# A chunked linear-attention stage fed into a SiLU feed-forward on one core: bonus sums, row casts and state rows reordered in the first six units, 128-column state sums, last rows in two halves

## The chip, the core and the metric

The kernel runs on one core of one Trainium2 chip. Its engines work side by side and meet at semaphores: TensorE (PE; its weight loads are shown apart, as PEld), VectorE (DVE), ScalarE (ACT), GpSimd (POOL) and SyncE (SP), which here only issues transfers. POOL issues transfers too, with a queue of its own. The metric is device microseconds of an execution, the median of several.

## What is computed

For each of 4 batches and 8 heads a 48x48 state runs over 768 time steps; its outputs, put side by side over the heads, go through a feed-forward of 384 to 2048 to 384 with a SiLU:

```python
for t in range(S):
    cur = einsum('bhd,bhe->bhde', u * k_t, v_t)
    y[:, :, t] = einsum('bhd,bhde->bhe', r_t, state + cur)
    state = w[..., None] * state + einsum('bhd,bhe->bhde', k_t, v_t)
x = y as (3072 rows, 384)
h = x @ w_in
out = (h * (1 / (1 + exp(-h)))) @ w_out
```

## The kernel before, in words

The 768 steps are cut into six chunks of 128; a unit is one chunk of one batch, so there are 24 units, unit i being chunk i // 4 of batch i % 4. Inside a unit the recurrence is written with matrices: r is multiplied by powers of w (lamR), k by inverse powers (lamK), both transposed so that the head dimension lies on partitions; a product of the two, masked to the strictly earlier steps, is multiplied by v; the state left by the chunks before is added by one more matmul; and the term with u (the bonus) is a row sum of r*k*u times v.

The names, in the order of a unit's work (lines of the kernel before):

- `nat_v` (L173, ACT) casts v to half precision. `nat_ku` (L178), `nat_rk` (L184) and `nat_kc` (L189), all on POOL, make k*u, r*k*u and k times w to the power of the steps left (lamC). `bonus_sum` (L195, DVE) sums r*k*u over the head dimension into rku, `bonus_vu` (L201, POOL) multiplies v by it. `bonus_act` (L205) is the same product done on ACT in eight pieces; nothing calls it in the kernel before.
- `p1` transposes r and k on PE into the PSUM tiles tr and tk (L221); DVE multiplies them by lamR and lamK into rk (L224, L228). From unit 4 on this is split in two: `p1t` (L240, into xs) and `p1d` (L251).
- `r16` (L257, ACT) casts the scaled r to half precision, for the matmul with the state.
- `p2` multiplies the two (L265 and L267, ae and ao, for even and odd heads); DVE masks both into am (L274). With `nxt` it also runs `p1t` of the next unit behind its matmuls and `p1d` behind its masks.
- `p3y` (L288, L291) makes y on PE, `p3e` (L298, DVE) adds vu; `p4` (L340) transposes y into yT, and ACT copies it into xT (L341).
- `sums` (L307) multiplies kc and v16 into the chunk's own state, sps. `state` (L316, L319 on DVE) adds it to the decayed one, and POOL makes sdec (L323) and, later, the half-precision state (L321). In chunks 0 and 1 that cast is `half_state` (L328, ACT).
- `l1` (L352, L355) is a tile of 128 hidden columns: three matmuls into hps, then a SiLU on ACT into gT. `l2` (L364) is a quarter of the 16 matmuls that make 128 rows of the output; behind the fourth quarter DVE copies (L368) and SP stores (L370).
- `to_cols` and `to_rows` turn a row of w or u into columns and spread columns over 128 rows. lamCT (L411, ACT) is turned into lamC by `to_rows`. `spin` issues matmuls on zeros.

Each engine runs its instructions in the order of the code, which is written out by hand. Units 0 to 5 are written one by one (L407 to L545), units 6 to 23 by the loop at L547. The feed-forward is cut into a list of fillers; `fill(n)` takes about n weights' worth from it (an `l1` over four batches or an `l2` quarter counts 1, an `l1` over two batches 0.5) and puts them between a unit's steps, so that PE has work while other engines finish. The last `fill(1000)` empties the list.

Transfers: SP loads r, k and v of each unit in 192 KB pieces, six units' worth of buffers. POOL issues w_in in four parts (L398) and w_out in two (L402); a memset into the buffer of unit 4 (L443), behind the last parts of w_in in POOL's queue, holds back the loads of unit 4 and all behind them. PSUM has five buffers for the attention's tiles, taken in turn, and three for hps and ops.

Of the kernel before, what the change touches and what calls it, by code (L numbers as in the profile page):

```python
# [8 lines left out]
FP = mybir.dt.float32  # L9
# [6 lines left out]
def kernel(  # L16
# [110 lines left out]
    def to_cols(row, copy):  # L127
        t = ps.tile([128, 512], FP, name="cols", tag="t", bufs=5)
        nc.tensor.transpose(t[0:PR, 0:NP], row.rearrange("p j d -> p (j d)")[:, 0:PR],
                            ident[0:NP, 0:NP])  # L130
        c = cst.tile([PR, NP], FP, name="cols_sb", bufs=2)
        copy(out=c, in_=t[0:PR, 0:NP])
        return c

    spin(5)
    wT = to_cols(wrow, nc.vector.tensor_copy)
    spin(5)
    u_bc = cst.tile([128, H, D], FP)
    lamC = cst.tile([128, H, D], FP)
# [1 line left out]
    def to_rows(dst, cols):  # L141

        t = ps.tile([128, NP, 2, 64], FP, name="rows", tag="t", bufs=5)
        for p in range(NP):
            nc.tensor.transpose(t[:, p, :, :].rearrange("t j d -> t (j d)")[:, 0:PR],
                                cols(p), ident[0:PR, 0:PR])
        nc.scalar.copy(out=dst.rearrange("t (p j) d -> t p j d", j=2), in_=t[:, :, :, 0:D])  # L147
# [22 lines left out]
    def nat_v(i):  # L170
        L = live.setdefault(i, {})
        L["v16"] = wrk.tile([128, H, D], F16, name="v16", bufs=6)
        nc.scalar.copy(out=L["v16"], in_=vin[i % NIN])  # L173
# [13 lines left out]
    def nat_kc(i):  # L187
        n = i % NIN
        nc.gpsimd.tensor_tensor(out=kc[i % NKC][:, :, 0:D], in0=kin[n][:, :, 0:D],  # L189
                                in1=lamC, op=ALU.mult)  # L190

    def bonus_sum(i):
        L = live[i]
        L["rku"] = wrk.tile([128, H], FP, name="rku", bufs=3)
        nc.vector.tensor_reduce(out=L["rku"], in_=L["rku_f"], axis=mybir.AxisListType.X,  # L195
                                op=ALU.add)

    def bonus_vu(i):
        L = live[i]
        L["vu"] = wrk.tile([128, H, D], FP, name="vu", bufs=3)  # L200
        nc.gpsimd.tensor_tensor(out=L["vu"], in0=vin[i % NIN],  # L201
                                in1=L["rku"].unsqueeze(2).broadcast_to([128, H, D]),
                                op=ALU.mult)
# [8 lines left out]
    def p1(i, mid=None, spins=0):  # L212
        n = i % NIN
        L = live.setdefault(i, {})
        tr = ps.tile([128, NP, C], FP, name="tr", tag="t", bufs=5)
        tk = ps.tile([128, NP, C], FP, name="tk", tag="t", bufs=5)
        spin(spins, tr)
        for t, src in ((tr, rin), (tk, kin)):
            flat = src[n].rearrange("p h d -> p (h d)")
            for p in range(NP):  # L220
                nc.tensor.transpose(t[0:PR, p, :], flat[:, 128 * p:128 * p + PR], ident)  # L221
        rk = wrk.tile([PR, 2, NP, C], FP, name="rk")
        L["rT"] = rk[:, 0]
        nc.vector.tensor_tensor(out=L["rT"], in0=tr[0:PR], in1=lamR, op=ALU.mult)  # L224
        if mid:
            mid()
        L["kT"] = rk[:, 1]
        nc.vector.tensor_tensor(out=L["kT"], in0=tk[0:PR], in1=lamK, op=ALU.mult)  # L228
# [27 lines left out]
        L["rT16"] = wrk.tile([PR, NP, C], F16, name="rT16")  # L256
        nc.scalar.copy(out=L["rT16"], in_=L["rT"])  # L257

    def p2(i, spins=0, nxt=None):
        L = live[i]  # L260
        ae = ps.tile([128, NP, C], FP, name="ae", tag="t", bufs=5)
        ao = ps.tile([128, NP, C], FP, name="ao", tag="t", bufs=5)
        spin(spins, ae)
        for p in range(NP):
            nc.tensor.matmul(ae[:, p, :], L["kT"][0:D, p, :], L["rT"][0:D, p, :],  # L265
                             start=True, stop=True)
            nc.tensor.matmul(ao[:, p, :], L["kT"][64:PR, p, :], L["rT"][64:PR, p, :],  # L267
                             start=True, stop=True)
        if nxt is not None:
            p1t(nxt)  # L270
        L["am"] = []
        for a in (ae, ao):
            am = wrk.tile([128, NP, C], F16, name="am", bufs=4)
            nc.vector.tensor_tensor(out=am, in0=a,  # L274
                                    in1=maskM.unsqueeze(1).broadcast_to([128, NP, C]),
                                    op=ALU.mult)
            L["am"].append(am)
        if nxt is not None:
            p1d(nxt)

    def p3y(i):
        sc, b = unit(i)
        L = live[i]
        v16 = L["v16"]
        L["y"] = y = ps.tile([128, H, D], FP, name="y", tag="t", bufs=5)
        for p in range(NP):
            if sc:
                nc.tensor.matmul(y[:, 2 * p:2 * p + 2, :], L["rT16"][:, p, :],  # L288
                                 st16[b][:, p, :], start=True, stop=False)
            for j in range(2):  # L290
                nc.tensor.matmul(y[:, 2 * p + j, :], L["am"][j][:, p, :],  # L291
                                 v16[:, 2 * p + j, :], start=not sc,
                                 stop=(not sc or j == 1))

    def p3e(i):
        L = live[i]
        L["y16"] = wrk.tile([128, H, D], F16, name="y16")
        nc.vector.tensor_tensor(out=L["y16"], in0=L["y"], in1=L["vu"], op=ALU.add)  # L298

    def sums(i):  # L300
        sc, b = unit(i)
        L = live[i]
        L["sps"] = sps = ps.tile([128, NP, PW], FP, name="sps", tag="t", bufs=5)
        kf = kc[i % NKC].rearrange("p h d -> p (h d)")
        vf = L["v16"].rearrange("p h d -> p (h d)")
        for p in range(NP):
            nc.tensor.matmul(sps[0:PR, p, :], kf[:, 128 * p:128 * p + PR],  # L307
                             vf[:, PW * p:PW * p + PW], start=True, stop=True)

    def state(i):  # L310
# [48 lines left out]
    def l2(sc, b, part):  # L359
# [6 lines left out]
        if part == 3:  # L366
# [2 lines left out]
            tt = b * S + sc * C  # L369
            nc.sync.dma_start(out=out[tt:tt + C, :], in_=osb)  # L370

    def l1s(sc, b0=0, b1=B):
        return [((b1 - b0) / B, lambda ft=ft: l1(sc, ft, b0, b1)) for ft in range(NFT)]

# [7 lines left out]
    def fill(n):  # L382
        owed[0] = min(owed[0] + n, n + 1.0)
        while fillers and owed[0] > 0.01:
            w_, f = fillers.pop(0)
            owed[0] -= w_
            f()
# [9 lines left out]
    def win_part(c0, c1):  # L397
        nc.gpsimd.dma_start(out=win[:, :, c0:c1],  # L398
                            in_=moe_w_in[:, c0:c1].rearrange("(q p) n -> p q n", p=128))
# [17 lines left out]
    nat_ku(0)  # L417
    nat_rk(0)
    p2(0)
    to_rows(lamC, lambda p: lamCT[:, p, :])  # L420
    bonus_sum(0)
    nat_ku(1)
    bonus_vu(0)
    nat_rk(1)
    p1(1, spins=3)
    p3y(0)
    p3e(0)
    nat_v(1)
    bonus_sum(1)
    win_part(512, 1024)  # L430
    bonus_vu(1)
    nat_kc(0)
    p2(1, spins=2)
    nc.scalar.copy(out=st[1], in_=zero)
    p4(0)
    p3y(1)
    p3e(1)
    p1(2)
    nat_ku(2)
    nat_rk(2)  # L440
# [7 lines left out]
    fillers.extend(l1s(0, 0, 2))  # L448
    fill(.5)
    nat_v(2)  # L450
    p2(2)
    bonus_sum(2)
    bonus_vu(2)
    nat_kc(1)
    fill(1.5)
    p3y(2)
    p3e(2)
# [2 lines left out]
    p4(2)  # L460
    nat_ku(3)
    nat_rk(3)
    nat_kc(2)
    nat_v(3)
    fill(1)
    p2(3)
    bonus_sum(3)
    bonus_vu(3)
    nc.scalar.copy(out=st[3], in_=zero)
    fill(2)  # L470
    p3y(3)
    p3e(3)
    a, b_ = B, B + 1
# [19 lines left out]
    fill(1)  # L493
    sums(0)
    state(0)
    half_state(0)
    nat_v(a)
    r16(a)
    nat_kc(a)
    fill(1)  # L500
    p2(a, nxt=b_)
    nat_ku(b_)
    nat_rk(b_)
# [3 lines left out]
    wout_part(0)  # L507
    sums(1)
    state(1)
    wout_part(1)  # L510
    fill(1)
    sums(a)
# [5 lines left out]
    nat_v(b_)  # L518
    for i in range(4):
        load(NIN + i)  # L520
    bonus_sum(b_)
    bonus_vu(b_)
    fill(1)
    p2(b_, nxt=b_ + 1)
    nat_kc(b_)
    fill(1.5)
    p3y(b_)
    p3e(b_)
    sums(2)
    state(2)  # L530
    load(NIN + 4)
    load(NIN + 5)
    fill(1)
    p4(b_)
    fillers.extend(l1s(1, 0, 2) + l2s(0))
    sums(b_)
    state(b_)
    fill(1)
    half_state(0)
    half_state(2)  # L540
    front(B + 2)
# [5 lines left out]
    for i in range(B + 2, NU):  # L547
        sc, b = unit(i)
        bonus_sum(i)
        bonus_vu(i)  # L550
        p2(i, nxt=i + 1 if i + 1 < NU else None)
        fill(2)
        if i + 1 < NU:
            front(i + 1)
            r16(i + 1)
        if i >= NIN:
            load(i + NIN)
        fill(1)
        p3y(i)
        p3e(i)  # L560
        if sc < NCH - 1:
            sums(i)
            state(i)
        fill(2)
        p4(i)
        if i == B + 2:
            half_state(3)
        fill(1)
        if sc == 1:
            half_state(b)  # L570
        fill(2)
        if b == B - 1:
            if sc == 1:
                fillers.extend(l1s(1, 2, 4) + l2s(1))
            else:
                fillers.extend(l1s(sc) + l2s(sc))
    fill(1000)

# [1 line left out]
_INS = ['r', 'k', 'v', 'w', 'u', 'moe_w_in', 'moe_w_out']  # L580
# [26 lines left out]
```

## Time and profile before

| | |
|---|---|
| median of 8 runs | 205.95 us (205.56 to 208.11) |
| the profiled execution | 206.05 us, of which span 204.3 us |
| granted TensorE clock | 1.00 |
| DVE, ACT, POOL busy | 115.2, 97.2, 116.0 us |
| first hps matmul, first ops matmul | 17.6, 51.1 us |
| last output copy on DVE | 200.62 to 201.18 us |

A row of the groups names the line, the engine, the operation, output <- inputs and their shapes, then how often it ran, its busy time in us and the mean of one in ns, and the idle time of its engine before it with what ended it. Matmuls are pipelined: the duration of one is longer than the distance from its start to the next one's start, and it is that distance that a row of them costs. Chains of work and waits are inferred from semaphore events.

### The profile page before, as it was taken

Reading aid. Unit: us, or ns where it says so; the run is one execution under the profiler, and the core shown is the slowest. Engines: PE = TensorE matmul, PEld = TensorE weight load, DVE = VectorE, ACT = ScalarE, POOL = GpSimd, SP = SyncE. Lnnn points to the kernel's source line nnn. Section 1 sums busy time; section 2 is a strip of 40 time slices with the busy share of each in tenths; the row PEclk is TensorE's granted clock in tenths of the full one; section 3 lists DMA queues with packets and bytes.
Section 4 is the critical chain, followed back from the end, with each engine's and each line's share of the span. In section 5 each row is a group of like instructions: output and inputs, shape, how many; then the busy total and the mean of one; then the engine's idle time right before and its main releaser. Section 6 shows DMA issues by size and latency. Waiting matters only on the chain.

```text
span 204.3 us, 4975 instructions
## 1 busy us (share of the span) xinstructions
PE 193.6 (95%) x1953; PEld 130.4 (64%) x1953; DVE 115.2 (56%) x233; ACT 97.2 (48%) x217; POOL 116.0 (57%) x146
## 2 busy tenths in 40 slices
PE   7988989988999999999999999999999999999992
PEld 2656768877667877675666765666765666644561
DVE  6786548958368548596447865546864635410121
ACT  2444567878431671129672119672119652069300
POOL 3498877989945954957774657571738370100000
PEclk9999999999999999999999999999999999999999
DMA  4999999999797920759731629201120001210022
GB/s 89 205 172 171 182 229 188 184 183 199 143 230 187 227 54 20 175 114 212 142 64 53 148 88 188 43 0 43 40 77 3 0 3 40 77 42 0 0 77 77
DMA packets 82063, 22.34 MB, mean 109 GB/s; under 512 B 75384, under 2 KB 82040, under 8 KB 82040
## 3 DMA queue, kind: packets, MB, share of 16 engines
q1 hardware_dynamic: 78360, 18.88, 42.8%
q0 software_dynamic: 3680, 3.15, 10.3%
q8 instruction: 15, 0.25, 0.5%
q14 instruction: 8, 0.07, 0.1%
HBM read 20.45 MB, written 4.72 MB: 123 GB/s over the span
## 4 chain that ended last, share of the span: by engine, by line
PE 76%; POOL 9%; DVE 6%; issue 5%; ACT 3%; POOLq 0%; ACTq 0%
PE ops L364 31%; PE hps L352 24%; PE ae L265 10%; PE xs L240 4%; POOL rku_f L184 2%; POOL ku L178 2%; PE yT L340 2%; PE y L291 2%; DVE rk L251 2%; PE sps L307 2%; DVE am L274 2%; PE y L288 1%; POOL win L398 1%; POOL vu L201 1%; ACT gT L355 1%
## 5 line engine op out<-in xcount | busy, mean ns | idle before, releaser
L352 PE MATMUL hps<-xT,win 128*128 128x256 f16 (+1 forms) x384 | 69.7, 326 | 1.7 <-ACT xT L341 0.9
L355 ACT ACTIVATE gT<-hps 128x256 f16<-128x256 f32 (+1 forms) x128 | 59.0, 493 | 23.2 <-PE hps L352 21.2
L364 PE MATMUL ops<-wout,gT 128*128 128x384 f16 x384 | 68.1, 326 | 0.0
L352 PEld LDWEIGHTS <-win 128*128 128x128 f16 x384 | 35.4, 98 | 23.7 <-issue 2.6
L364 PEld LDWEIGHTS <-gT 128*128 128x128 f16 x384 | 35.8, 98 | 22.2
L274 DVE TENSOR_TENSOR am<-ae,maskM 128x512 f16<-128x512 f32 x24 | 16.6, 691 | 38.4 <-PE ao L267 38.2
L201 POOL TENSOR_TENSOR vu<-vin,rku 128x384 f32<-128x384 f32 x24 | 19.9, 830 | 22.2 <-DVE rku L195 22.0
L368 DVE COPY osb<-ops 128x384 f32<-128x384 f32 x24 | 13.3, 556 | 31.7 <-PE ops L364 31.5
L257 ACT CAST rT<-rk 112x512 f16<-112x512 f32 x20 | 12.4, 619 | 37.6 <-DVE rk L251 37.6
L265 PE MATMUL ae<-rk 48*128 48x128 f32 x192 | 27.7, 285 | 0.5 <-DVE rk L228 0.5
L265 PEld LDWEIGHTS ae<-rk 48*128 48x128 f32 x192 | 23.1, 187 | 7.7 <-issue 5.3
L267 PE MATMUL ao<-rk 48*128 48x128 f32 x192 | 27.7, 285 | 0.0
L251 DVE TENSOR_TENSOR rk<-xs,pif 112x512 f32<-112x512 f32 x40 | 25.6, 680 | 1.7 <-PE xs L240 1.7
L184 POOL TENSOR_TENSOR rku_f<-rin,ku 128x384 f32<-128x384 f32 x24 | 24.1, 1004 | 1.8
L178 POOL TENSOR_TENSOR ku<-kin,u_bc 128x384 f32<-128x384 f32 x24 | 24.0, 1002 | 0.2 <-ACT u_bc L147 0.2
L189 POOL TENSOR_TENSOR kc<-kin,lamC 128x384 f16<-128x384 f32 x24 | 24.1, 1002 | 0.0
L341 ACT COPY xT<-yT 128x384 f16<-128x384 f16 x24 | 11.5, 479 | 25.6 <-PE yT L340 25.6
L267 PEld LDWEIGHTS ao<-rk 48*128 48x128 f32 x192 | 23.1, 187 | 0.0
L321 POOL CAST stb<-st 112x384 f16<-112x384 f32 x12 | 6.0, 504 | 25.8 <-DVE st L316 25.8
L298 DVE TENSOR_TENSOR y<-y,vu 128x384 f16<-128x384 f32 x24 | 13.3, 553 | 7.8 <-PE y L291 5.8
L274 DVE TENSOR_TENSOR am<-ao,maskM 128x512 f16<-128x512 f32 x24 | 16.3, 680 | 0.0
L323 POOL TENSOR_TENSOR sdec<-st,pif 112x384 f32<-112x384 f32 x16 | 13.4, 838 | 3.3 <-DVE st L316 2.7
(71 smaller groups left out, 183.8 us busy)
## 6 DMA issues: line engine op xcount, KB each, us to landing
rin<-in_r_dram SPq DMA_DIRECT2D x24, 192.0 KB, 3.4
kin<-in_k_dram SPq DMA_DIRECT2D x24, 192.0 KB, 3.7
vin<-in_v_dram SPq DMA_DIRECT2D x24, 192.0 KB, 3.6
out_dram<-osb SPq DMA_DIRECT2D x24, 192.0 KB, 2.0
win<-in_moe_w_in_dram POOLq DMA_DIRECT2D x4, 384.0 KB, 6.2
wout<-in_moe_w_out_dram POOLq DMA_DIRECT2D x2, 768.0 KB, 12.6
wrow<-in_w_dram SPq DMA_DIRECT2D x1, 1.5 KB
urow<-in_u_dram SPq DMA_DIRECT2D x1, 1.5 KB
```

The source lines that it names most:

```text
L178: nc.gpsimd.tensor_tensor(out=L["ku"], in0=kin[i % NIN][:, :, 0:D], in1=u_bc, op=ALU.mult)
L184: nc.gpsimd.tensor_tensor(out=L["rku_f"], in0=rin[i % NIN][:, :, 0:D], in1=L["ku"], op=ALU.mult)
L189: nc.gpsimd.tensor_tensor(out=kc[i % NKC][:, :, 0:D], in0=kin[n][:, :, 0:D], in1=lamC, op=ALU.mult)
L201: nc.gpsimd.tensor_tensor(out=L["vu"], in0=vin[i % NIN], in1=L["rku"].unsqueeze(2).broadcast_to([128, H, D]), op=ALU.mult)
L251: nc.vector.tensor_tensor(out=rk[:, :, :, 64 * g:64 * g + 64], in0=xs[g][0:PR], in1=lam(g), op=ALU.mult)
L265: nc.tensor.matmul(ae[:, p, :], L["kT"][0:D, p, :], L["rT"][0:D, p, :], start=True, stop=True)
L267: nc.tensor.matmul(ao[:, p, :], L["kT"][64:PR, p, :], L["rT"][64:PR, p, :], start=True, stop=True)
L274: nc.vector.tensor_tensor(out=am, in0=a, in1=maskM.unsqueeze(1).broadcast_to([128, NP, C]), op=ALU.mult)
L323: nc.gpsimd.tensor_tensor(out=sdec[b], in0=st[b], in1=wCT.unsqueeze(2).broadcast_to([PR, NP, PW]), op=ALU.mult)
L352: nc.tensor.matmul(hps, win[:, q, ft * 128:(ft + 1) * 128], xts[sc][:, q, b0:b1, :].rearrange("p b t -> p (b t)"), start=(q == 0), stop=(q ...
L355: nc.scalar.activation(out=gts[sc][:, ft, b0 * C:b1 * C], in_=hps, func=AF.Silu)
L364: nc.tensor.matmul(ops, gts[sc][:, ft, b * C:(b + 1) * C], wout[:, ft, :], start=(ft == 0), stop=(ft == NFT - 1))
```

## The change

It touches five things.

1. The first six units are put into another order. p1(1) runs straight behind p2(0), with one spin in front instead of three; lamC's rows are made behind p3y(0). vu of unit 0 is made by ACT (`bonus_act`) instead of POOL, and its p3e comes behind p2(1) and bonus_sum(1). In units 2 and 3 `bonus_sum` and `bonus_vu` stand ahead of `p2`, so that DVE sums before it masks; nat_kc(1) moves down to unit 3. In unit 3 the fillers stand otherwise around the steps. For unit 5 (`b_`), bonus_sum, bonus_vu and nat_kc move up, ahead of the second part of w_out; its `p2` runs with `late=True`, which leaves `p1d` of unit 6 to be called behind p3e(5). half_state(0) moves behind the first SiLUs; fills of .5 replace some of 1.
2. In the loop, `r16` of the next unit moves from ahead of p3y to behind p4.
3. `sums` loads 128 weight columns instead of 112 and writes 128 partitions of sps. The 16 added columns are the zero padding of kc.
4. wT is read by DVE from PSUM, without the copy.
5. The last 128 rows of output are made in two halves of 192 columns, each with its own copy and store (`l2_last`).

```diff
-        c = cst.tile([PR, NP], FP, name="cols_sb", bufs=2)
+        if copy is None:
+            return t[0:PR, 0:NP]
+        c = cst.tile([PR, NP], FP, name="cols_sb")
...
-    wT = to_cols(wrow, nc.vector.tensor_copy)
+    wT = to_cols(wrow, None)
...
-    def p2(i, spins=0, nxt=None):
+    def p2(i, spins=0, nxt=None, late=False):
...
-        if nxt is not None:
+        if nxt is not None and not late:
             p1d(nxt)
...
-            nc.tensor.matmul(sps[0:PR, p, :], kf[:, 128 * p:128 * p + PR],
+            nc.tensor.matmul(sps[:, p, :], kf[:, 128 * p:128 * p + 128],
...
+    def l2_last(sc, b):
+
+        tt = b * S + sc * C
+        for n0 in (0, HD // 2):
+            ops = ps.tile([128, HD], FP, name="ops", tag="moe", bufs=3)
+            for ft in range(NFT):
+                nc.tensor.matmul(ops[:, 0:HD // 2], gts[sc][:, ft, b * C:(b + 1) * C],
+                                 wout[:, ft, n0:n0 + HD // 2],
+                                 start=(ft == 0), stop=(ft == NFT - 1))
+            osb = wrk.tile([128, HD // 2], FP, name="osh")
+            nc.vector.tensor_copy(out=osb, in_=ops[:, 0:HD // 2])
+            nc.sync.dma_start(out=out[tt:tt + C, n0:n0 + HD // 2], in_=osb)
...
     p2(0)
-    to_rows(lamC, lambda p: lamCT[:, p, :])
+    p1(1, spins=1)
     bonus_sum(0)
     nat_ku(1)
-    bonus_vu(0)
     nat_rk(1)
-    p1(1, spins=3)
+    nat_v(1)
     p3y(0)
+    to_rows(lamC, lambda p: lamCT[:, p, :])
+    bonus_act(0)
+    nc.scalar.copy(out=st[1], in_=zero)
+    win_part(512, 1024)
+    p2(1, spins=2)
+    bonus_sum(1)
+    bonus_vu(1)
     p3e(0)
-    nat_v(1)
-    bonus_sum(1)
-    win_part(512, 1024)
-    bonus_vu(1)
     nat_kc(0)
-    p2(1, spins=2)
-    nc.scalar.copy(out=st[1], in_=zero)
-    p4(0)
     p3y(1)
     p3e(1)
+    p4(0)
     p1(2)
...
     nat_v(2)
-    p2(2)
     bonus_sum(2)
     bonus_vu(2)
-    nat_kc(1)
+    p2(2)
     fill(1.5)
...
     p4(2)
     nat_ku(3)
     nat_rk(3)
+    fill(1)
+    bonus_sum(3)
+    nat_kc(1)
     nat_kc(2)
+    bonus_vu(3)
+    p2(3)
+    nc.scalar.copy(out=st[3], in_=zero)
+    fill(1)
     nat_v(3)
     fill(1)
-    p2(3)
-    bonus_sum(3)
-    bonus_vu(3)
-    nc.scalar.copy(out=st[3], in_=zero)
-    fill(2)
     p3y(3)
...
     sums(0)
     state(0)
-    half_state(0)
     nat_v(a)
     r16(a)
     nat_kc(a)
-    fill(1)
+    fill(.5)
+    half_state(0)
+    fill(.5)
     p2(a, nxt=b_)
...
     sums(1)
     state(1)
+    bonus_sum(b_)
+    bonus_vu(b_)
+    nat_kc(b_)
     wout_part(1)
...
-    bonus_sum(b_)
-    bonus_vu(b_)
-    fill(1)
-    p2(b_, nxt=b_ + 1)
-    nat_kc(b_)
-    fill(1.5)
+    fill(.5)
+    p2(b_, nxt=b_ + 1, late=True)
+    fill(1)
     p3y(b_)
     p3e(b_)
+    p1d(b_ + 1)
     sums(2)
     state(2)
     load(NIN + 4)
     load(NIN + 5)
-    fill(1)
+    fill(.5)
     p4(b_)
+    fill(1.5)
     fillers.extend(l1s(1, 0, 2) + l2s(0))
     sums(b_)
     state(b_)
-    fill(1)
+    fill(.5)
...
             front(i + 1)
-            r16(i + 1)
...
         p4(i)
+        if i + 1 < NU:
+            r16(i + 1)
...
+    del fillers[-4:]
     fill(1000)
+    l2_last(NCH - 1, B - 1)
```

## The prediction

> **What bounds the kernel.** I read first the busy shares and slices of the page, then the table of time windows, then who made TensorE wait, then the instructions in order of time around those waits.
>
> ```profile
> PE 193.6 (95%) x1953; PEld 130.4 (64%) x1953; DVE 115.2 (56%) x233; ACT 97.2 (48%) x217; POOL 116.0 (57%) x146
> ...
> PE   7988989988999999999999999999999999999992
> ...
> DMA  4999999999797920759731629201120001210022
> ```
> ```profile
> 30.00:53.00 23.00, 21.04 (x277) 17.69 (x274) 16.72 (x35) 18.54 (x51) 21.02 (x25) 1.00 1.07 179
> 53.00:200.60 147.60, 147.48 (x1449) 95.41 (x1447) 78.86 (x148) 64.38 (x130) 73.17 (x85) 1.00 0.37 87
> ```
>
> In the windows the second number is the length, the third TensorE's busy time, the last three its granted clock, the DMA share and GB/s. After 53 us TensorE is busy for 147.48 of 147.60: there only cheaper matmuls help. Before 53 us it idles, and there (from slice 2 to about 51 us) the DMA engines are full too. TensorE's waits between 14 and 75 us:
>
> ```profile
> PE yT L340 <- DVE y L298: 1.8, 2, 1.0
> PE y L291 <- DVE am L274: 1.2, 3, 0.5
> PE hps L352 <- ACT xT L341: 0.9, 2, 0.6
> PE hps L352 <- ACT gT L355: 0.7, 1, 0.7
> ```
>
> In order of time, measured from start to start against the usual pace, they are 0.57 at 15.0, 0.73 at 16.8, 0.42 at 20.1, 0.16 and 0.27 at 22.2 and 23.3, 1.06 at 27.0, 0.23 at 33.8, 1.05 at 40.3, 0.47 at 41.8, 0.14 at 47.0, 0.86 at 49.0, and 0.26 at 72.9. The last cases are typical: a product or a SiLU is late because its engine is first held by something not urgent.
>
> ```profile
> 39.58 1.28 DVE L251 TENSOR_TENSOR rk<-xs,pif 112x512 f32<-112x512 f32 x2
> ...
> 40.77 0.55 DVE L298 TENSOR_TENSOR y<-y,vu 128x384 f16<-128x384 f32 x1
> ...
> 41.37 0.34 PE L340 MATMUL yT<-ident,y 128*128 128x128 f16 x3 [0.89 <-DVE y L298]
> ```
> ```profile
> 49.03 0.62 ACT L257 CAST rT<-rk 112x512 f16<-112x512 f32 x1 [0.52 <-DVE rk L251]
> ...
> 49.99 1.14 PE L352 MATMUL hps<-xT,win 128*128 128x256 f16 x9 [0.70 <-ACT gT L355]
> ```
>
> One fact limits all of this. The second half of w_out is issued at 37.98 and takes 14.4 us, so it lands at 52.4; the ninth ops matmul, the first that needs it, starts at 52.47, 0.04 late against the pace of 0.162. Whatever TensorE gains before that point, it gains only if w_out comes earlier too.
>
> ```profile
> L402 POOL DMA_DIRECT2D wout<-in_moe_w_out_dram x2: 937/937/937, 36.2 to 38.0; - x2
> ...
> DMA to landing us min/median/max: 10.8/12.6/14.4
> ```
>
> **State sums.** From the groups by line:
>
> ```profile
> L288 PEld LDWEIGHTS <-rT 112*128 112x128 f16 x80 | 7.7, 96 | 1.4
> ...
> L307 PEld LDWEIGHTS <-kc 128*112 128x112 f16 x80 | 5.8, 130 | 0.1
> ```
>
> A load of 112 columns takes 130 ns, one of 128 takes 96. Four sps matmuls take 0.22 us start to start (64.73 to 64.95), 55 ns each. Loads of 128 columns don't set the pace: 384 moving columns take 162 ns, 256 take 109, so 0.414 ns a column, and 96 columns should take 43; the y group at 64.44 has 96 + 48 + 48 columns in 0.10 us, which fits. Saving (55 - 43) x 4 = 0.05 us a unit, 1.0 for 20 units, 0.65 for the 13 units after 52.5 us. [...]
>
> **Start.** The copy of wT that goes (0.16) gives nothing: DVE then waits longer for tr, which stands behind the spins until 5.79. p1(1) now follows p2(0): rin and kin of unit 1 are there, one spin and eight transposes run from 9.2 to 10.2, DVE scales rk(1) right after the am pair, done at 11.85 (before 13.03), and ae(1) starts at 11.95 instead of 13.08. But rku(1), formerly ahead of the am pair at 13.56, is now behind it: am to 14.4, rku to 14.9, vu on POOL (0.83) to 15.8, y to 16.4, yT, then xT (0.48): hps at 17.4 instead of 17.61. Gain 0.2. The eight ACT scalings of vu(0) have no row; lamCT (128 columns) goes at 0.32 each, sil (one column) at 0.20: 1.6 to 2.6, I take 2.0, from 12.4 to 14.4. DVE asks at 14.8, so it is covered at 2.0 and costs up to 0.2 at the top. The later rku(1) leaves POOL idle until 14.9: ku and rku_f of unit 2, win parts 3 and 4 and the memset that releases the loads of unit 4 slip by 0.6 (win from 18.08 to 18.7). SP's own order is unchanged but for the split last store. The DMA engines had run out of other work there, so kin of unit 4 lands at 27.4 instead of 26.8 (issued 20.20, 6.6 us).
>
> **Units 2 and 3.** rku(2) ahead of am(2) waits for rku_f(2), 18.8, ends at 19.4; am ends at 20.6, as before. TensorE waits 0.7 instead of 0.42, but vu(2) is done at 21.2 instead of 21.9, y(2) at 21.85, and the gaps of 0.16 and 0.27 close. For unit 3 POOL does ku, rku_f (23.3), kc twice and then vu, 25.15 to 26.0 (before 26.74 to 27.57), with rku at 23.9 no longer behind am. y(3) is done at 26.75, and the gap of 1.06 is gone. xs(4) starts at 27.6 instead of 29.14: 1.5 gained so far.
>
> **Units 4 to 6.** POOL can't follow: ku(4) waits for kin until 27.5, as before. What POOL gains is the 1.09 us it waited for rku(4): ku, rku_f, kc to 30.5, vu, sdec, kc, ku, rku_f to 35.1, then w_out part 0 at 35.1 instead of 36.24. Part 1 stands behind sdec, vu(5) and kc(5), at 38.6 instead of 37.98; part 0 is then still moving (it landed 10.8 us after its issue), so it loses nothing. On TensorE: half_state(0) behind the first SiLUs removes the 0.23; p1d(6) behind y(5) with three hps on each side leaves about 0.5 of the 1.05 + 0.47 (y(5) itself waits 0.3 for am, having one hps group less ahead, and sps(5) now waits for the PSUM buffer that rk(6) frees at 39.6); hps of the second chunk start at 39.85 instead of 42.28. Then am(6) is late: rku(6) waits for rku_f(6), at 44.6 (before 45.85), since sdec three times and ku(6) stand ahead of it; am ends at 46.4 and TensorE waits 1.1. r16(7) behind yT(6) removes the 0.86. The first ops would start at 48.8, and the ninth at 50.1.
>
> **w_out.** Both parts move one behind the other in POOL's queue; 36.24 to 52.4 is 16.2 us. Issued at 35.1, the second half lands at 51.3. So TensorE waits about 1.2 us, and 1.15 of the gain before this point survives (52.47 - 51.35). Nothing where w_out moves as late as before; 2.35 where it isn't waited for.
>
> **After 52.5 us.** Sums 0.65. r16 behind yT: the 0.26 at 72.9; the next unit's y needs it only three fills later. **Last rows:** 32 matmuls of 192 columns at 82 ns for 16 at 162: +0.03. [...] The last copy falls from 0.556 to about 0.35 (the 48x192 copies), its store by 0.1 of 1.9 us (estimated: half the bytes, same latency; bounds 0 and 0.3). Sum 0.3 gained.
>
> **Sum.** 1.15 + 0.65 + 0.26 + 0.3 = 2.35 off the profiled execution's 206.05 (span 204.3 and 1.7 around it): 203.7. The median of the eight runs is 205.95, 0.1 below it; the forecast stays 203.7.
>
> **Rivals.** First, w_out isn't the limit: its packets come sooner, since the transfer of loads of units 6 to 8 in front of it is short. For it: in the DMA records at 41 to 48 us the two queues take turns packet by packet (about 193 each per us), and w_out alone at 39 to 41 was no faster (182 to 185), so company costs it nothing. Against: 16.2 us from issue to landing at a full DMA. Then 2.35 + 1.2 = 3.55 are gained: 202.5. Second, w_out lands as late as before, because it shares the engines with loads of unit 8 that had landed earlier in the run before: 1.2 remains, 204.8. Third, slower: w_out part 1 now stands behind vu(5) and so behind rku(5) and the state copies on DVE. While part 0 moves this is free, and a part that has nothing ahead of it takes 10.8 us (part 0). So from an issue at 41.6 on it lands later than the 52.4 of before, and at 43.9 it lands at 54.7: 2.2 lost against 1.2 gained, 207.0, and more beyond. I put the issue at 38.6; it takes a slip of 5.3, and the three steps ahead of it are 2.7 long. Fourth, that the 128-column load isn't the fast one: 0.65 less; the row of L288 has the same engine, type and width, so I count it inside the others.
>
> **Chances.** Forecast 0.5 (203.0 to 204.3), first rival 0.23 (201.9 to 203.0), second 0.2 (204.3 to 205.4), slower 0.07. The range of 202.2 to 205.2 leaves out the slower case, and a tenth at the ends of the others. A measurement tells 0.5%, 1.03 us, from no change: faster means below 204.9. That is the forecast, the first rival and about half of the second, 0.83; within 0.11; slower 0.06.
>
> **What would show it.** sps loads near 98 ns and four matmuls in 0.17 us; first hps near 17.4; xs(4) near 27.6; no wait of hps for gT near 49 and 73; w_out issued near 35.1 and 38.6; a stall before the ninth ops matmul of about 1.2 us, at 50 to 51.4. I am wrong if that stall is missing, if POOL reaches w_out much later, or if ACT's scalings of vu(0) hold DVE past 15 us.

## The result and the profile after

The changed kernel takes 203.83 us (median of 11 executions, 203.63 to 205.38) against 206.29 for the kernel before (32 executions beside it); the ratio is 0.9891, interval 0.9863 to 0.9919. The forecast was 203.7. The profiled execution takes 203.83 us with a span of 202.1.

In part of the executions of nearly every kernel here the granted clock of TensorE falls near 15 us (to 0.50 for 3.41 or 6.83 us in the five profiled ones of them), and the time is longer (205.35 us against 203.81 for the changed kernel); a number "at the full clock" is the median of those executions whose mean granted clock is at least 0.995, and "a fall" below is a mean under 0.985. At the full clock the changed kernel takes 203.81 (8 executions). The kernel before takes 205.90, 205.87 and 206.26 on the three chips of the experiments (the first four of them, the next four, the last four), so a difference of 0.4 us between kernels on different chips can be the chip's.

The page's busy shares and the slices of TensorE and DMA:

```profile
PE 192.4 (95%) x1967; PEld 130.5 (65%) x1967; DVE 115.2 (57%) x233; ACT 97.9 (48%) x225; POOL 115.1 (57%) x145
...
PE   7977999998999999999999999999999999999993
...
DMA  4997999999998911769631739201120001210022
```

The early slices are still not full, and the DMA engines are as busy as before until about 50 us. TensorE's waits from 14 to 75 us, as engine, line and name, the one waited for, the sum in us, the number and the longest:

```profile
PE y L293 <- DVE am L276: 2.5, 6, 0.8
PE yT L342 <- DVE y L300: 0.8, 2, 0.6
PE hps L354 <- ACT xT L343: 0.6, 1, 0.6
PE hps L354 <- ACT gT L357: 0.4, 1, 0.4
PE y L293 <- ACT v L175: 0.2, 1, 0.2
```

The waits for DVE's y fell from 1.8 to 0.8 and those for SiLUs from 0.7 to 0.4, but those for DVE's masks rose from 1.2 to 2.5, and a wait for v is new. No wait for a transfer is in the list. The w_out view says why:

```profile
L417 POOL DMA_DIRECT2D wout<-in_moe_w_out_dram x2: 937/937/937, 35.5 to 39.0; - x2
...
DMA to landing us min/median/max: 8.9/9.8/10.7
```

The second half, issued at 39.03, lands 10.7 us later, at 49.7. The ninth ops matmul starts at 51.14, one normal step (0.163) behind the eighth. Before, the two issues were 1.7 us apart and the second half took 14.4.

The state sums in the groups by line:

```profile
L309 PE MATMUL sps<-v,kc 128*128 128x96 f16 x80 | 6.6, 204 | 0.0
L309 PEld LDWEIGHTS <-kc 128*128 128x128 f16 x80 | 4.4, 96 | 0.1
```

A load takes 96 ns instead of 130, and four matmuls 0.167 us from start to start instead of 0.221.

Where the 2.2 us between the two profiled executions came from, cut at TensorE's marks (us gained in each stretch; `spins_in_gap` is an experiment below, in which the clock is steady):

| stretch | predicted | changed kernel | spins_in_gap |
|---|---|---|---|
| to the first hps matmul | 0.2 | -0.1 (17.61 to 17.69) | 0.2 |
| from there to xs of unit 4 | 1.3 | 0.8 (11.53 to 10.76) | 1.1 |
| from there to the ninth ops matmul | -0.4 | 0.6 (23.33 to 22.69) | 0.6 |
| from there to the start of the last copy | 0.9 | 0.4 (148.15 to 147.74) | 0.4 |
| from there to the span's end | 0.3 | 0.5 (3.73 to 3.23) | 0.5 |

The sum was right to 0.1 us; the terms were not. With the spins the gain is 2.8 and not 2.2.

### The profile page after: what moved, and what is told of

It reads as the page before. It is cut to its first block, busy times and chain, and to the rows that moved or that the text cites. A ratio compares the mean times of both kernels' runs of the same rounds, so it can differ in the third digit from the quotient of the medians.

```text
span 202.1 us, 5004 instructions
## 1 busy us (share of the span) xinstructions
PE 192.4 (95%) x1967; PEld 130.5 (65%) x1967; DVE 115.2 (57%) x233; ACT 97.9 (48%) x225; POOL 115.1 (57%) x145
## 4 chain that ended last, share of the span: by engine, by line
PE 80%; POOL 7%; issue 5%; DVE 4%; ACT 2%; POOLq 0%; DVEq 0%
PE ops L366 30%; PE hps L354 27%; PE ae L267 10%; PE xs L242 4%; PE y L293 3%; DVE am L276 2%; POOL rku_f L186 2%; POOL ku L180 2%; PE yT L342 2%; PE y L290 2%; PE sps L309 1%; PE ops L380 1%; DVE y L300 1%; POOL win L413 1%; ACT gT L357 1%
## 5 line engine op out<-in xcount | busy, mean ns | idle before, releaser
L357 ACT ACTIVATE gT<-hps 128x256 f16<-128x256 f32 (+1 forms) x128 | 59.6, 494 | 25.6 <-PE hps L354 23.8
L366 PE MATMUL ops<-wout,gT 128*128 128x384 f16 x368 | 65.5, 326 | 0.0
L354 PEld LDWEIGHTS <-win 128*128 128x128 f16 x384 | 35.1, 98 | 22.5 <-issue 1.6
L366 PEld LDWEIGHTS <-gT 128*128 128x128 f16 x368 | 34.2, 98 | 21.1
L203 POOL TENSOR_TENSOR vu<-vin,rku 128x384 f32<-128x384 f32 x23 | 19.1, 830 | 19.7 <-DVE rku L197 19.7
L370 DVE COPY osb<-ops 128x384 f32<-128x384 f32 x23 | 12.8, 556 | 29.2 <-PE ops L366 29.0
L197 DVE TENSOR_REDUCE rku<-rku_f 128x8 f32<-128x384 f32 x24 | 13.2, 550 | 4.7 <-POOL rku_f L186 4.3
L293 PE MATMUL y<-v,am 128*128 128x48 f16 x192 | 12.5, 185 | 3.0 <-DVE am L276 2.7
```

The lines of the kernel that those rows point to most:

```text
L203: nc.gpsimd.tensor_tensor(out=L["vu"], in0=vin[i % NIN], in1=L["rku"].unsqueeze(2).broadcast_to([128, H, D]), op=ALU.mult)
L293: nc.tensor.matmul(y[:, 2 * p + j, :], L["am"][j][:, p, :], v16[:, 2 * p + j, :], start=not sc, stop=(not sc or j == 1))
L354: nc.tensor.matmul(hps, win[:, q, ft * 128:(ft + 1) * 128], xts[sc][:, q, b0:b1, :].rearrange("p b t -> p (b t)"), start=(q == 0), stop=(q ...
L357: nc.scalar.activation(out=gts[sc][:, ft, b0 * C:b1 * C], in_=hps, func=AF.Silu)
L366: nc.tensor.matmul(ops, gts[sc][:, ft, b * C:(b + 1) * C], wout[:, ft, :], start=(ft == 0), stop=(ft == NFT - 1))
```

## The experiments

**The 128-column sums by themselves** (`sums128_alone`), in the kernel before:

```diff
-            nc.tensor.matmul(sps[0:PR, p, :], kf[:, 128 * p:128 * p + PR],
+            nc.tensor.matmul(sps[:, p, :], kf[:, 128 * p:128 * p + 128],
```

> The kernel before with only the 128-column state sums. Theory (TensorE's pace is the cost): four sps matmuls take 0.17 us instead of 0.22, so 0.05 us for each of the 13 units behind 52.5 us, 0.7 us in all, and up to 1.0 if the seven earlier units count too: 205.2 (205.0 to 205.4) against 206.0 for the kernel before. Rival (w_out's landing holds the ops stage in every execution): the earlier seven are lost, 205.3. Rival (a load of 128 columns is no faster in this place): 206.0.

Measured: 205.49, ratio 0.9959 (0.9933 to 0.9986); at the full clock 205.34 against 205.90 on the same chip, 0.56 less. The stretch from the ninth ops matmul to the last matmul is 0.65 shorter (147.78 to 147.13), which is 13 units of 0.05. The load and the pace are those of the changed kernel. So the column count is the cause. That the seven earlier units are lost to w_out is not told apart: the time fits 0.56 to 0.7 better than 1.0, and the ninth ops matmul starts here just behind the landing, at 52.09 against 52.05.

**The row cast in the loop, put back** (`r16_old_place`), in the changed kernel:

```diff
             front(i + 1)
+            r16(i + 1)
...
         p4(i)
-        if i + 1 < NU:
-            r16(i + 1)
```

> The changed kernel, with the half-precision cast of the next unit's rows in the loop put back ahead of p3y. Prediction's theory: the cast holds SiLUs at 49 us (0.86) and 72.9 us (0.26), so the time rises by 1.0 to 204.8. Theory from the trace of after: the cast behind the copy of xT makes a new wait of 0.5 us near 66 us in place of the 0.26, so putting it back costs 0.9 at 49 us and gives 0.25 back later: 204.4. Rival: DVE's mask of unit 6 is late anyway, so the wait at 49 us is only partly added: 203.8 to 204.0.

Measured: 205.86, ratio to the kernel before 0.9953 (0.992 to 0.9986); at the full clock 204.82, 1.0 more than the changed kernel. In order of time:

```profile
48.75 0.62 ACT L259 CAST rT<-rk 112x512 f16<-112x512 f32 x1 [1.96 <-DVE rk L253]
49.28 1.99 ACT L357 ACTIVATE gT<-hps 128x256 f16<-128x256 f32 x6
49.70 1.14 PE L354 MATMUL hps<-xT,win 128*128 128x256 f16 x9 [1.20 <-ACT gT L357]
```

ACT idles 1.96 us for DVE's rk with SiLUs behind the cast, and TensorE waits 1.2 us for them. The prediction's mechanism is shown, and it is worth more here than the 0.86 of before, because TensorE arrives earlier. The 1.0 is less than the 1.36 lost at this place: the rest is given back later, as the next run shows.

**The row cast still later** (`r16_after_fills`): behind the last fillers of an iteration.

```diff
         p4(i)
-        if i + 1 < NU:
-            r16(i + 1)
...
         fill(2)
+        if i + 1 < NU:
+            r16(i + 1)
```

> The changed kernel, with that cast behind all fillers of the iteration instead of straight behind p4. Theory (two ACT casts in a row outlast the three hps buffers, one alone doesn't): the waits near 66 us and near 73 us are both gone, 0.5 us less than the changed kernel: 203.3. Rival (a cast costs TensorE the same wherever SiLUs are being made): no change, 203.8. Rival (the cast is now late for the next unit's y): slower, 204.3 or more.

The time can't be read here: in 5 of 6 executions the clock fell, and the one at the full clock took 203.11. The trace of the changed kernel has the wait, and this one has not. The changed kernel:

```profile
65.18 0.48 ACT L343 COPY xT<-yT 128x384 f16<-128x384 f16 x1 [5.75 <-PE yT L342]
65.56 0.62 ACT L259 CAST rT<-rk 112x512 f16<-112x512 f32 x1
...
66.07 1.67 ACT L357 ACTIVATE gT<-hps 128x256 f16<-128x256 f32 x5
66.51 0.82 PE L354 MATMUL hps<-xT,win 128*128 128x256 f16 x6 [0.39 <-ACT gT L357]
```

With the cast behind the fillers:

```profile
66.42 1.83 PE L354 MATMUL hps<-xT,win 128*128 128x256 f16 x15
66.62 0.48 ACT L343 COPY xT<-yT 128x384 f16<-128x384 f16 x1 [5.75 <-PE yT L342]
67.00 1.68 ACT L357 ACTIVATE gT<-hps 128x256 f16<-128x256 f32 x5
68.57 0.61 ACT L259 CAST rT<-rk 112x512 f16<-112x512 f32 x1
```

The xT copy and the cast behind one another hold ACT for 0.9 us (65.18 to 66.07), and TensorE, with three hps buffers of 0.33 us each (three matmuls 0.109 us apart), waits 0.39 us for a SiLU; behind either of them alone, 0.5 us for the copy and 0.6 for the cast, it does not. The prediction counted only that the cast leaves the place near 73 us, not what stands beside it in the new one.

**The second half of w_out late** (`wout_part1_late`):

```diff
     nat_kc(b_)
-    wout_part(1)
...
     sums(b_)
     state(b_)
+    wout_part(1)
     fill(.5)
```

> The changed kernel, with the second half of w_out issued behind the states of units 4 and 5 on POOL, near 43.5 us instead of 39.0. Theory (a part lands 10.7 us after its own issue, the ninth ops matmul waits for it): it lands at 54.2, TensorE waits 3.1 us there, and little of it comes back: 206.8. Rival (landing follows the first part's issue, 16.2 us behind it): 51.7, a wait of 0.6, 204.4. Rival (the two queues are served by what is left, and the bulk is through near 49.5 us anyway): no wait, 203.8.

Measured: 206.52 (22 executions, in 12 of which the clock fell), ratio 0.9951 (0.992 to 0.9981); at the full clock 204.86, 1.05 more. All three guesses of size are off. In the profiled execution, one with the fall, the half issued at 45.25 lands 7.9 us later, 0.7 us ahead of its use. The first half, with no other moving beside it either, took 9.4. So a half by itself lands 8 to 9.4 us after its issue and not 10.8, which the third rival had assumed; as a transfer its price would have been lower still. The loss comes from POOL. The issue keeps POOL for 0.94 us, and it now stands straight ahead of the products of unit 6:

```profile
45.25 0.94 POOL L417 DMA_DIRECT2D wout<-in_moe_w_out_dram  x1
...
47.30 1.00 POOL L186 TENSOR_TENSOR rku_f<-rin,ku 128x384 f32<-128x384 f32 x1
```

`r16_after_fills`, which has the same fall and the same xs of unit 4 (29.89 and 29.88), makes that product 1.28 us earlier:

```profile
46.02 1.00 POOL L186 TENSOR_TENSOR rku_f<-rin,ku 128x384 f32<-128x384 f32 x1
```

Its ninth ops matmul starts 1.28 us earlier as well (52.58 against 53.86), and TensorE waits 0.9 us there for DVE's masks instead of 2.2. So in this order of units 4 to 6 the bonus product of unit 6 on POOL sets when TensorE gets to the ops matmuls.

**The old order of units 0 and 1** (`start_old`), in the changed kernel: p1(1) behind the bonus of unit 0 with three spins, vu(0) on POOL, the sum of unit 1 ahead of its masks.

```diff
     p2(0)
-    p1(1, spins=1)
+    to_rows(lamC, lambda p: lamCT[:, p, :])
     bonus_sum(0)
     nat_ku(1)
+    bonus_vu(0)
     nat_rk(1)
+    p1(1, spins=3)
...
-    bonus_act(0)
...
+    bonus_sum(1)
...
     p2(1, spins=2)
```

> The changed kernel with the old order of units 0 and 1 (row product of unit 0 on POOL, bonus sum of unit 1 ahead of its masks, three spins). Theory A (the new start leaves TensorE nearly idle from 12.6 to 15.1 us, and that is what lets its granted clock fall to half from about 15 to 21 us in part of the executions): at the full clock within 0.4 us of the changed kernel, 203.6 to 204.2, and fewer executions with the fall, about as few as of the kernel before. Theory B (the prediction's: the new start gains 0.2 and does nothing to the clock): 204.0, the fall as frequent as in the changed kernel.

Measured: 204.12 (6 executions), ratio 0.989 (0.983 to 0.995); at the full clock 203.17 (3 executions, 202.98 to 204.18), too few, and on another chip, to call it faster than the changed kernel. In none was the mean clock under 0.985, but in 3 of 6 it was 0.992, so the old start has a drop as well, a shorter one (0.50 for 3.41 us in the profiled execution).

**The old order of units 2 and 3** (`mid_old`): masks ahead of bonus sums; v of unit 3 is cast earlier too, as in the kernel before.

```diff
+    p2(2)
     bonus_sum(2)
     bonus_vu(2)
-    p2(2)
+    nat_kc(1)
...
-    fill(1)
+    nat_kc(2)
+    nat_v(3)
+    fill(1)
+    p2(3)
     bonus_sum(3)
-    nat_kc(1)
-    nat_kc(2)
     bonus_vu(3)
-    p2(3)
...
-    fill(1)
-    nat_v(3)
-    fill(1)
+    fill(2)
```

> The changed kernel with the old order of units 2 and 3: masks ahead of bonus sums. Theory A (this part took away the wait for y of unit 3): xs of unit 4 starts about 1 us later, and nearly all of it stays, since w_out lands 1.4 us ahead of need in the changed kernel: 204.7 at the full clock. Theory B (w_out's landing takes the gain back): w_out is issued up to 1 us later and its landing decides, 204.3 or less. Theory C (loads of unit 4 decide): no change, 203.8.

Measured: 205.93 (22 executions, in 14 of which the clock fell), ratio 0.9959 (0.993 to 0.9989); at the full clock 204.39, 0.6 more than the changed kernel. From the first hps to xs of unit 4 it takes 12.82 us with the fall, against 11.66 in `r16_after_fills`, which has the same start and the same fall: 1.2 us for this part, and the wait for y of unit 3 is back:

```profile
PE yT L342 <- DVE y L300: 1.2, 2, 1.0
PE y L293 <- DVE am L276: 0.9, 3, 0.4
```

In the profiled execution all of it is still there at the ninth ops matmul (53.81 against 52.58); at the full clock 0.6 is left. What takes the other half there is not shown. Here w_out, issued at 38.15 and 41.63, lands at 53.77 and the ninth ops matmul starts at 53.81, 0.07 late: the issue moves with this part, as the prediction held.

**The old order around unit 5** (`unit5_old`): the product of unit 5 behind the scaling of unit 6, its bonus behind both halves of w_out, half_state(0) ahead of the SiLUs.

```diff
     state(1)
-    bonus_sum(b_)
-    bonus_vu(b_)
-    nat_kc(b_)
     wout_part(1)
...
-    fill(.5)
-    p2(b_, nxt=b_ + 1, late=True)
-    fill(1)
+    bonus_sum(b_)
+    bonus_vu(b_)
+    fill(1)
+    p2(b_, nxt=b_ + 1)
+    nat_kc(b_)
+    fill(1.5)
     p3y(b_)
     p3e(b_)
-    p1d(b_ + 1)
```

> The changed kernel with the old order from the first state sum to the second fillers: bonus sum of unit 5 late, scaling of unit 6 ahead of y of unit 5, half_state(0) ahead of the SiLUs. Theory A (the waits of 1.05 and 0.47 us come back in place of 0.37 and 0.23): 0.9 slower, 204.7 at the full clock. Theory B (the sum of unit 6 waits for POOL anyway and takes up what was gained before it): 203.8 to 204.1.

Measured: 204.58 (22 executions, in 11 of which the clock fell), ratio 0.9908 (0.9877 to 0.9938); at the full clock 203.64, within 0.2 of the changed kernel. The part gains nothing. TensorE's waits between 30 and 56 us in this kernel:

```profile
PE yT L342 <- DVE y L300: 0.9, 1, 0.9
PE ops L366 <- DMA wout<-in_moe_w_out_dram: 0.4, 1, 0.4
PE hps L354 <- ACT xT L343: 0.3, 1, 0.3
```

And the same place in the changed kernel, where the masks of unit 6 are the last to come:

```profile
46.48 0.21 PE L290 MATMUL y<-stb,rT 112*128 112x96 f16 x1
46.94 0.20 PE L293 MATMUL y<-v,am 128*128 128x48 f16 x1 [0.25 <-DVE am L276]
47.54 0.20 PE L293 MATMUL y<-v,am 128*128 128x48 f16 x1 [0.40 <-DVE am L276]
```

DVE can't mask unit 6 before it has summed its bonus, and POOL makes that product only at 44.6 to 45.6:

```profile
45.61 0.55 DVE L197 TENSOR_REDUCE rku<-rku_f 128x8 f32<-128x384 f32 x1 [2.31 <-POOL rku_f L186]
46.20 0.69 DVE L276 TENSOR_TENSOR am<-ae,maskM 128x512 f16<-128x512 f32 x1
```

Whatever TensorE gains around unit 5, it waits for there. The new order even makes that product later: 16.1 us behind xs of unit 4, where it starts 15.6 us behind it in `unit5_old`, and the eighth ops matmul comes 22.5 us behind xs against 22.1. What the new order gives in return is an earlier w_out. In `unit5_old` the halves are issued 1.7 us apart at 35.90 and 37.64 and land last at 51.59; the ninth ops matmul, due at 51.1, starts at 51.63. It is the one profiled execution with such a wait (0.54; nowhere else is it over 0.1), and here the stall that was predicted exists. So two limits lie close together, and this part exchanges one for the other.

**Spins in the gaps of the start** (`spins_in_gap`). Where the clock rises early, TensorE has little but the eight short matmuls of y(1) from about 12.6 to 15.1 us. This run adds eight matmuls on zeros there, into a buffer that nothing uses yet.

```diff
     nat_kc(0)
+    spinm(3)
     p3y(1)
     p3e(1)
+    spinm(5)
     p4(0)
```

> The changed kernel with eight matmuls on zeros in the two gaps of TensorE ahead of y of unit 1 and of yT of unit 0. Theory A (the clock falls because TensorE is idle there): no execution with the fall, and the same time at the full clock, 203.8. Theory B (the fall comes at random, or from earlier): as often as in the changed kernel. Theory C (the matmuls delay y): up to 0.3 slower at the full clock.

Measured: 203.22 (5 executions, 203.18 to 203.89), ratio 0.9857 (0.9812 to 0.9902), and no fall. The same windows in two kernels, with start and end, length, TensorE's busy time, the other engines, then granted clock, DMA share and GB/s. `r16_after_fills`:

```profile
12.60:15.10 2.50, 0.78 (x14) 0.38 (x10) 2.21 (x4) 1.83 (x8) 1.38 (x3) 0.98 1.15 220
15.10:21.00 5.90, 5.30 (x34) 4.38 (x35) 2.50 (x4) 2.15 (x5) 5.82 (x9) 0.50 0.79 130
```

`spins_in_gap`:

```profile
12.60:15.10 2.50, 2.07 (x21) 0.89 (x18) 2.21 (x4) 1.83 (x8) 1.43 (x3) 1.00 1.21 209
15.10:21.00 5.90, 5.07 (x57) 4.07 (x56) 3.62 (x7) 3.19 (x8) 5.82 (x9) 1.00 0.89 148
```

With TensorE busy 0.78 of 2.5 us the clock is 0.50 for the next six; with 2.07 it stays at 1.00, and 57 matmuls are done there instead of 34. Over all kernels run here with the new start and without the spins, the clock fell in 55 of 110 executions, with the spins in 0 of 23: the spins end it. In the kernel before it fell in 27 of 111. That the new start makes falls more frequent is not shown by this: the changed kernel itself has 2 of 12, and on one chip `start_new_alone` has 4 of 12 and the kernel before 3 of 17.

In these traces the drop stands at a fixed distance behind the rise. `r16_after_fills` from the rise of its clock on, then the low stretch of `start_old` (the columns are those above):

```profile
4.74:14.98 10.24, 7.60 (x79) 5.54 (x77) 7.96 (x15) 5.83 (x19) 6.07 (x8) 1.00 1.11 206
14.98:21.81 6.83, 6.11 (x38) 4.95 (x39) 3.34 (x7) 2.15 (x5) 6.75 (x9) 0.50 0.81 130
21.81:30.00 8.19, 7.91 (x92) 6.46 (x92) 4.61 (x8) 6.17 (x19) 6.39 (x8) 1.00 1.17 211
...
15.15:18.56 3.41, 2.84 (x21) 2.37 (x18) 2.40 (x4) 0.89 (x2) 3.33 (x5) 0.50 1.02 163
```

The traces' clock records have the rise at 4.66 to 5.13 us in all five profiled executions with a low stretch, the drop 10.24 us behind it, and the return 3.41 or 6.83 us later: all multiples of 3.41. In the profiled executions without spins in which it rose later (at 5.80, 6.38, 6.43 and 7.40; `r16_old_place` has no record of it) the clock stayed up. With the spins it rose at 4.19 and 4.76 in two executions and stayed up as well. So in the nine traces without spins that have these records the drop goes with an early rise, and the little work from 12.6 to 15.1 us is what the spins take away.

**The two halves of w_out back to back** (`wout_back_to_back`), from `spins_in_gap`:

```diff
     wout_part(0)
+    wout_part(1)
     sums(1)
...
-    wout_part(1)
```

> spins_in_gap, with the second half of w_out issued straight behind the first on POOL (near 35.9 us instead of 38.4), so that vu and kc of unit 5 come one issue, 1 us, later. Theory A (two halves issued close together have stragglers: the last piece lands about 16 us behind the first issue, as in the kernel before): it lands near 50.9 us, the ninth ops matmul (50.5) waits up to 0.4: 203.2 to 203.6. Theory B (a half lands about 11 us behind its own issue or the queue's bulk): 47 to 49 us, no wait, 203.2. If y of unit 5 waits for its later vu: up to 0.5 more in either theory.

Measured: 203.29 (6 executions), ratio 0.9845 (0.9808 to 0.9882), the same as `spins_in_gap` (203.22 on another chip). Issued at 36.05, the second half lands at 50.61, 15.5 us behind the first issue (35.11) and 1 us later than when it was issued 2.4 us later; the ninth ops matmul starts at 50.72 with a normal step. This is theory A's landing without its wait.

**The new start by itself** (`start_new_alone`): in the kernel before, the lines of `start_old` the other way round.

> The kernel before with only the new order of units 0 and 1. Theory A (the new start itself lets the clock fall): at least half of the executions show a granted clock under 0.99, against about a third of the kernel before; at the full clock 0.3 to 0.7 slower than the kernel before, 206.2 to 206.6, since start_old was that much faster than the changed kernel. Theory B (the prediction's 0.2 gain at the start, kept in part behind w_out): 205.7 to 206.0, and no more falls than the kernel before.

Measured: 206.58 (12 executions), ratio 1.0005 (0.9973 to 1.0037); at the full clock 205.93 against 206.26 on the same chip, 0.3 less; under 0.985 in 4 of 12 executions (3 of 17 for the kernel before). At the full clock theory B is right and theory A's 0.3 to 0.7 slower wrong; taken over all executions the gain and the falls cancel.

**The last rows in one piece** (`last_rows_whole`), from `spins_in_gap`: without the call of `l2_last` and the cut of the fillers.

```diff
-    del fillers[-4:]
     fill(1000)
-    l2_last(NCH - 1, B - 1)
```

> spins_in_gap, with the last 128 rows made in one piece again, as in the kernel before. Prediction's theory: 0.3 slower, 203.5. Theory from the traces (copy's start to the end 0.44 less, matmuls 0.03 more): 0.4 slower, 203.6. Rival (the two stores hinder each other, or loads show): no change, 203.2, or faster.

Measured: 203.68, ratio 0.9873 (0.983 to 0.9915); 0.46 more than `spins_in_gap`, which ran on another chip. The traces say the same: from the start of the last copy to the span's end 3.74 us against 3.22, with 0.04 less before it. The 192-column matmuls start 82.5 ns apart in the changed kernel, so the added loads hide.

**The best version found** (`cast_late_v3_early_spins`): `spins_in_gap` with the cast of `r16_after_fills`, and v of unit 3 cast ahead of two SiLUs.

```diff
     nat_rk(3)
+    nat_v(3)
     fill(1)
...
-    fill(1)
-    nat_v(3)
-    fill(1)
+    fill(2)
```

> spins_in_gap, with the cast of the next unit's rows behind the iteration's last fillers and v of unit 3 cast one step earlier on ACT. Theory: the wait of 0.5 near 66 us goes, and y of unit 3 no longer waits for v16 (0.28 at 25.3 us), of which w_out may take a part: 202.5 to 202.8. Rival (each cast holds back SiLUs wherever it is put): 203.2.

Measured: 202.58 (6 executions, 202.41 to 202.99), ratio to the kernel before 0.9813 (0.9775 to 0.9851): faster than both kernels. All that TensorE waits for from 12 us to the end of this kernel:

```profile
PE y L299 <- DVE am L282: 1.6, 5, 0.4
PE hps L360 <- ACT xT L349: 0.6, 1, 0.6
PE yT L348 <- DVE y L306: 0.2, 1, 0.2
```

The waits for SiLUs and for v are gone.

## Why the prediction was right, and where it was not

The number was right with luck: in the profiled execution of the changed kernel the clock rose late, at 7.40 us (6.43 before), and without that and the falls, with the spins, the kernel takes 203.22, 0.5 below the forecast.

**State sums: right.** 0.05 us a unit, 0.65 behind 52.5 us; the trace has 13 x 0.054 = 0.70, the time of the edit alone 0.56. The load of 128 columns takes 96 ns where that of 112 took 130, and the four matmuls 0.167 us where they took 0.221.

**Start: right in the order of things, wrong in what it left out.** ACT's eight scalings took 1.9 us where I took 2.0, and DVE did not wait for them. With the clock rising at the same time the first hps matmul comes 0.3 earlier than before (17.29 in `start_new_alone`, rise at 6.38; 17.61 before, rise at 6.43), 0.2 predicted. But the step said nothing of TensorE's clock, and that is worth as much: in `sums128_alone`, with the old start and a rise at 5.80, the first hps matmul comes at 17.30. In the profiled execution of the changed kernel the eight transposes of unit 0 start 0.213 us apart up to 7.3 us, where before only the first three did and the later ones 0.11. That is 0.4 us, and it is not made up: from the first product of unit 0 to xs of unit 4 it takes 19.9 us here and with the spins. The other change of the clock, the drop, came in `r16_after_fills` at 14.98 us, with TensorE idle for 1.72 us of the 2.50 from 12.60 to 15.10; the last gap, up to 15.14, was 0.58 long.

**Units 2 and 3: right in mechanism, a term too large.** The wait of 1.06 for y of unit 3 went, as predicted. Up to xs of unit 4 the first two rows of the table are better read together, since the spins move the mark between them: 1.5 predicted, 0.7 in the changed kernel, 1.3 with the spins. I had missed that v of unit 3 is now cast behind two SiLUs on ACT. In order of time in the changed kernel:

```profile
26.44 0.36 PE L293 MATMUL y<-v,am 128*128 128x48 f16 x8 [0.22 <-ACT v L175]
```

With v cast earlier, `cast_late_v3_early_spins` has xs of unit 4 at 27.58 (27.6 predicted) instead of 27.84.

The loads of unit 4 came late for POOL, as predicted: ku(4) waits 1.6 us for kin and starts at 27.9 (27.5 predicted).

**w_out: the step that failed.** The prediction put it: "So TensorE waits about 1.2 us". It waited for nothing. Two sizes were off and met from both sides. The transfer took 14.2 us from the first issue (35.53, predicted 35.1) to the last landing, instead of the 16.2 carried over from before. That figure belonged to halves issued 1.7 us apart and is not fixed even there: `start_new_alone` has 15.3. And TensorE came to the ninth ops matmul at 51.14, not 50.1. So the number that came out for this point, 51.35, was right to 0.2 for a wrong reason. Nearly all of TensorE's delay stood at xs of unit 4 already (28.45, predicted 27.6): 0.4 of it is the clock, 0.3 the wait for v, and the rest is open. From xs on it takes 22.69 us, and 22.5 was predicted without a stall. In that stretch the wait at the masks of unit 6 was rightly counted (1.1 predicted, 0.99 from start to start); as `wout_part1_late` shows, this chain of POOL and DVE through the bonus product of unit 6 sets TensorE's time there, not a transfer. With the old order of unit 5 the transfer would have, so the part changed what limits, and gained nothing to within 0.2 us.

The rival in which w_out isn't the limit named the right fact and the wrong time: its 202.5 knew of no late clock, no wait for v and no new wait near 66 us. `cast_late_v3_early_spins`, which is without these three, takes 202.58.

**The row cast: the gain near 49 us right, the later one reversed.** Predicted 0.86 and 0.26. In the changed kernel's surroundings the first is 1.36 (1.2 of it as a wait for SiLUs), and the second is a loss: 0.55 near 66 us in place of 0.26 near 73 us, about -0.3. That makes the stretch behind the ninth ops matmul 0.4 instead of 0.9.

**Last rows: right in mechanism, too small.** 0.50 from the copy's start to the span's end instead of 0.3: the copy 0.20 less, as predicted, and the store lands 1.62 us after its issue instead of 1.85. `last_rows_whole` gives 0.46. The copy of wT, which was put at nothing, has no run of its own; the first transpose of unit 0 starts at 5.79 before and after.

The slower rival did not come near: the second half of w_out was issued at 39.03 (38.6 predicted).

## What to carry to other kernels

When one wait of an engine is taken away, look for the next operation on the same chain that another engine makes late, and value the edit by the distance to that one; two edits ahead of the same late operation do not add, and an edit may make that operation later. An operation moved to a "free" place on an engine should be judged with its new neighbours, since buffers may cover one of them but not two: near 66 us three hps buffers of 0.33 us covered the copy of xT alone (0.48 us), and not the copy with the cast behind it (0.9). Gaps close together on TensorE can cost more than their length: with TensorE busy for 0.78 of 2.5 us the clock was 0.50 behind them (`r16_after_fills`), and executions of the changed kernel with a fall took 205.35 us against 203.81. The eight matmuls on zeros were cheap: 203.22 with them, and no fall in 23 executions.

## What the runs showed of the hardware that was not expected

- The granted clock fell to 0.50 behind 2.5 us in which TensorE was busy for 0.78 (`r16_after_fills`; 1.45 in `start_old`), at a price of about 1.5 us (205.35 against 203.81 for the changed kernel). The drop came 10.24 us behind the clock's rise and lasted 3.41 or 6.83 us, and of the profiled executions without spins those five had it in which the clock rose at 5.13 us or earlier.
- How long w_out took went with how its halves were issued. From the first issue to the last landing: 15.3 to 16.2 us in the five kernels with 0.9 to 1.7 us between the issues, 14.1 to 14.8 in six of the eight with 3.5 us between them (15.3 and 15.6 in the other two), and the last piece came 0.6 to 3.5 us behind the first. What holds the last pieces was not found.
- A half of w_out with no other half moving landed in 7.9 and 9.4 us (`wout_part1_late`), a first half with a second behind it in 8.7 to 10.8, a second half behind a first in 10.6 to 14.6.
